# Weight operands of the second layer pair made once during the first, and Strassen's scheme for both products of all three pairs of blocks

## The chip, the cores and the metric

The kernel runs on one core of a Trainium2 chip. The metric is the device time of one execution in microseconds (us); lower is better. TensorE (PE) does the matrix products, VectorE (DVE), ScalarE (ACT) and GpSimd (POOL) the elementwise work, and SyncE (SP) issues the DMAs. Each engine works through its own list of instructions strictly in the order in which they were written into it; between engines, semaphores are waited on.

## The reference

```python
def reference(...):          # attention, then two feed-forward layers over 3072 tokens
    attn_out = _attn_ref(q, k, v, mem_k, mem_v)      # B=4, H=8, S=768, D=64; chunks of 32 with context and 8 memory keys
    x = attn_out.transpose(0, 2, 1, 3).reshape(B * S, H * D)          # 3072 x 512
    h = x @ moe_w_in                                                  # 512 -> 2048
    x = (h * clip(h + 3, 0, 6) / 6) @ moe_w_out                       # 2048 -> 512
    h = x @ moe2_w_in
    return maximum(0.01 * h, h) @ moe2_w_out
```

The weights come in as 64-bit floating point numbers, which the kernel decodes to 32-bit ones itself. Every 32-bit operand of a product is split into a high and a low part, and a product takes three matrix instructions: high by high, low weights by high, high by low.

## The kernel before

All work is in feature-major layout: a tile has 128 features on its partitions and 512 tokens in its row. The 3072 tokens are six blocks of 512. The first feed-forward layer goes block by block and, within a block, over 16 slices f of 128 hidden features. For each f, `hidden` issues 12 matmuls into a bank `h` (L647); then ACT writes the gate into `r` (L660), DVE multiplies (L663), ACT casts the high part of `g` (a call of `copy`, L291), and POOL or DVE subtracts to get the low part (`minus`, L294). `output` then issues 12 matmuls over the four banks `y` (L695) for the slice f - 1. So PE alternates: `h` of f + 1, `y` of f, `h` of f + 2, `y` of f + 1, each 12 matmuls of 512 columns. At a block's end `y_out` takes the four banks to SBUF tiles `ys` and writes them to the DRAM tensor `spill`. All 32 decoded and split weight tiles of the first layer stay in SBUF; the pool `w` has 33 places. While the first layer runs, the attention of later blocks is interleaved with it, and so is the decoding of the second layer's weights: `to_dram` decodes a slice (one ACT and four DVE instructions, L352 to L367) and writes it to DRAM.

The second layer takes the blocks in three pairs. Strassen's scheme (Winograd's form) computes a product of 2 x 2 blocks with seven block products instead of eight; its left operands are the three weight blocks a11, a12, a22 and four sums s1 to s4, its right operands three blocks of x and four sums t1 to t4 (`x_pair`, `x_quarter`). `seven` is the first product in this scheme for one pair p and one pair i of hidden slices, seven products of 6 matmuls (L977). `second` is the second product in the same scheme (L1114). Before the change `second` serves pairs 1 and 2 only: pair 0 uses `output` for both of its blocks, 12 matmuls for each block and each f. Pair 0 also makes the weight operands: `w_set` loads two decoded slices, forms the four sums and splits all seven operands, which pair 0 uses at once and which `keep` also writes to the DRAM tensor `kept` for the pairs 1 and 2; `w_more` does the same for the sums of the second product's weights during the first layer, and `w_static` writes their plain blocks during pair 0. Pairs 1 and 2 read each operand from `kept` through a ring of six `w` tiles (`left`).

The order on every engine is set before the launch by `schedule`: a list scheduler that plays the program through with assumed durations, lets each engine take the ready task with the lowest key, and gives out buffers as they come free in that play. Keys count matmuls in groups of four; a first-layer step f has 6 of them, and its `r` and `g` tasks have a key 12 below the step's own. A task whose key lies lower than that goes ahead of them.

```python
for f in range(KF):
    w32["2i", f] = to_dram("2i", w2i, f, B0 + 1.25 * BLK + 24 * f)
    w32["2o", f] = to_dram("2o", w2o, f, B0 + 1.25 * BLK + 24 * f + 12)
    if f % 2:
        w_more(f // 2, B0 + 1.25 * BLK + 24 * f + 32)
```

Of the kernel before, what the change touches and what calls it, by code (L numbers as in the profile page):

```python
# [35 lines left out]
N = 512  # L36
# [172 lines left out]
def tile_attn_moe_moe2(ctx: ExitStack, tc: tile.TileContext, raw, w1i, w1o, w2i, w2o, out):  # L209
# [41 lines left out]
    w2 = {n: dram.tile([KF, 128, 512], F32, name="w32" + n) for n in ("2i", "2o")}  # L251
    later = dram.tile([NT // (2 * N), KF, 128, N], F32, name="later")
# [59 lines left out]
    for p in range(PAIRED):  # L312
        if p:
            for i in range(KF // 2):
                seq2 += [("p", p, i, n) for n in FIRST]
                if i == 0 and p == 1:
                    seq2.append(("y", 1, KF - 1))
                seq2 += [("p", p, i, n) for n in THEN]
            seq2 += [("q", p, n, i) for n in FIRST + THEN for i in range(KF // 2)]
            continue  # L320
        for i in range(KF // 2):
            seq2 += [("p", p, i, n) for n in FIRST]
            if i == 0:
                seq2.append(("y", 2 * p - 1, KF - 1))
            else:
                seq2.append(("y", 2 * p, 2 * i - 2))
            seq2 += [("p", p, i, n) for n in THEN]
            if i:
                seq2.append(("y", 2 * p, 2 * i - 1))
        seq2 += [("y", 2 * p, KF - 2), ("y", 2 * p, KF - 1)]  # L330
        seq2 += [("y", 2 * p + 1, f) for f in range(KF - 1)]
    at = STEP * len(items)
    for kind, j, *of in seq2:
        if kind in "pq":
            (pos_p if kind == "p" else pos_q)[(j, *of)] = at
            at += 1.5
        else:
            if j >= 0:
                pos_y["2", j, of[0]] = at
            at += 3  # L340

    wbuf, wtask, w32 = {}, {}, {}

    def decode(src, f, key, early=None, after=(), place="wm"):
# [25 lines left out]
        k = add(absolute, {"ACT": act(512)}, key, after=[k], allocs=[m], uses=[t])  # L370
# [240 lines left out]
    wlast, ylast, ghi, rs = {}, {}, [], []  # L614
# [8 lines left out]
    def two_parts(lay, j, f, r, k, key, low, i=None):  # L623
        g = Buf("g")

        def of():
            return r.t if i is None else r.t[:, i]

        k = add(lambda e: copy(e, make(g)[:, 0, :], of()), {"ACT": act(N), "DVE": dve2(N)}, key, after=[k, *(ghi[-1:] if lay == "2" else [])], allocs=[g], uses=[r])
        ghi.append(k)  # L630
        k2 = add(lambda e: minus(e, g.t[:, 1, :], of(), g.t[:, 0, :].bitcast(F32)), low, key, after=[k], uses=[r, g])
        gbuf[lay, j, f, 0], gtask[lay, j, f, 0] = g, (k, k2)

    def hidden(lay, j, f, c0, n):
# [22 lines left out]
        wlast.setdefault((lay, "i", f), []).append(k)  # L657
# [17 lines left out]
    def output(lay, j, f, c0, n):  # L675
        t0 = blocks[j][0]

        halves = (KF // 2, KF) if lay == "1" and j < TWICE else (KF,)
        begin = c0 == 0 and f in (0, *halves)
        end = f + 1 in halves  # L680
        if begin:
            ybuf[lay, j] = banks_of(lay == "2" and (j // 2 + j) % 2 == 1)
# [26 lines left out]
        wlast.setdefault((lay, "o", f), []).append(ks[-1])  # L709
        ylast[lay, j, f] = ks[-1]  # L710
# [5 lines left out]
    def y_out(lay, j, f, t0, n, d, y, k, two):  # L716
        s = Buf("ys")
        key = pos_y[lay, j, f] - 12
        scale = 1.0 / 6.0 if lay == "1" else 1.0
        dst = (out if lay == "2" else spill)[d, :, t0:t0 + n]  # L720
# [15 lines left out]
        else:  # L736
            k = add(take, {"DVE": dve(n)} if d % 2 else {"ACT": act(n, 50.0)}, key, after=[k], allocs=[s], uses=[y])
# [77 lines left out]
    wop, wdone, chain, kdone = {}, {}, [], {}  # L815
# [7 lines left out]
    def sums_of(raws, sums, at, l, key):  # L823

        def part(name):
            if name in at:
                c, o = at[name]
                return raws[c].t[:, o:o + 256]
            c, o = {"s1": (0, 0), "s2": (0, 256), "s3": (1, 0), "s4": (1, 256)}[name]
            return sums[c].t[:, o:o + 256]  # L830

        def form(out, x, y, op, after, allocs=(), uses=()):
            def fn(e):
                for b in allocs:
                    make(b, ([128, 512], F32))
                engine(e).tensor_tensor(out=part(out), in0=part(x), in1=part(y), op=op)
            return add(fn, {"DVE": dve(256)}, key, after=after, allocs=allocs, uses=[*raws, *uses])

        s1 = form("s1", "a21", "a22", ALU.add, l, allocs=sums[:1])
        s2 = form("s2", "s1", "a11", ALU.subtract, [s1, l[0]], uses=sums[:1])  # L840
        s3 = form("s3", "a11", "a21", ALU.subtract, l, allocs=sums[1:])
        s4 = form("s4", "a12", "s2", ALU.subtract, [s2, s3], uses=sums)
        return s1, s2, s3, s4

    def load_raws(which, i, raws, key, after=()):
        out = []
        for c in range(2):
            def fn(e, c=c):
                nc.sync.dma_start(out=make(raws[c]), in_=w2[which][2 * i + c])
            out.append(add(fn, {"SP": dma(262144, 330.0)}, key, after=[w32[which, 2 * i], w32[which, 2 * i + 1], *after], allocs=[raws[c]]))  # L850
        return out

    def w_set(p, i, key):


        raws = [Buf("wm"), Buf("wm")]
        sums = [Buf("st"), Buf("st")]
        ts = [Buf("w") for _ in range(4)]
        gate = [pk[p, i - 1, 1]] if i else []
        l = load_raws("2i", i, raws, key - 16, chain)  # L860
        s1, s2, s3, s4 = sums_of(raws, sums, {"a11": (0, 0), "a12": (0, 256), "a21": (1, 0), "a22": (1, 256)}, l, key)

        def two(t, src, n, after):
            def fn_hi(e):
                make(ts[t], ([128, 2, 2, 256], F32R))
                copy(e, ts[t].t[:, 0].rearrange("p o c -> p (o c)")[:, :n], src.t[:, 512 - n:])

            def fn_lo(e):
                v = ts[t].t.rearrange("p h o c -> p h (o c)")
                minus(e, v[:, 1, :n], src.t[:, 512 - n:], v[:, 0, :n].bitcast(F32))  # L870

            hi = add(fn_hi, {"ACT": act(n)}, key + 0.5, after=after + gate, allocs=[ts[t]], uses=[src])
            lo = add(fn_lo, {"DVE": dve(n)}, key + 0.6, after=[hi], uses=[src, ts[t]])
            return hi, lo

        wop[p, i] = ts
        wdone[p, i] = d = [two(0, raws[0], 512, [l[0]]), two(1, sums[0], 512, [s1, s2]), two(2, sums[1], 512, [s3, s4]), two(3, raws[1], 256, [l[1]])]
        for q, n in enumerate(ORDER):
            c, o = IN_W[LEFT_OF[n]]
            keep("i", 7 * i + q, lambda c=c, o=o: ts[c].t[:, :, o], d[c], [ts[c]], key + 12)  # L880

    def w_more(i, key):


        raws = [Buf("wm"), Buf("wm")]
        sums = [Buf("ys"), Buf("ys")]
        l = load_raws("2o", i, raws, key - 8, chain)
        made_ = sums_of(raws, sums, {"a11": (0, 0), "a21": (0, 256), "a12": (1, 0), "a22": (1, 256)}, l, key)
        chain.clear()
        for q, n in enumerate(ORDER):  # L890
            name = LEFT_OF[n]
            if name[0] != "s":
                continue
            v = int(name[1]) - 1
            t, src, o = Buf("st"), sums[v // 2], 256 * (v % 2)

            def fn_hi(e, t=t, src=src, o=o):
                copy(e, make(t, ([128, 2, 256], F32R))[:, 0], src.t[:, o:o + 256])

            def fn_lo(e, t=t, src=src, o=o):  # L900
                minus(e, t.t[:, 1], src.t[:, o:o + 256], t.t[:, 0].bitcast(F32))

            hi = add(fn_hi, {"ACT": act(256)}, key + 0.5, after=[made_[v]], allocs=[t], uses=[src])
# [45 lines left out]
    def seven(p, i, n):  # L949


        if (p, i) not in held:
            held[p, i] = banks_of(p == 0 or i % 2), Buf("w"), {}
# [35 lines left out]
        if p:  # L989
            rlast[m] = [k]  # L990
# [305 lines left out]
```

## Time and profile before

| what | us |
|---|---|
| median of 3 runs (lowest, highest) | 1104.91 (1103.12, 1108.45) |
| time of the profiled execution | 1105.37 |
| its span, first to last instruction | 1103.6 |
| PE busy in the span | 1067.1 (97%) |
| DVE busy | 665.9 (60%) |
| ACT busy | 513.9 (47%) |
| POOL busy | 112.6 (10%) |
| DMA queue of the program, share of 16 engines | 59.7% |

The profile is of one execution. Its time is 1.8 us longer than its span and 0.5 us above the median. In rows of the timeline the first number is the start and the second the duration of an instruction, both in us; what is in square brackets is how long the engine stood idle before it and which instruction ended that. The duration of an instruction reaches until its results are written, and the next one on the same engine may start before that.

### The profile page before, as it was taken

How to read it: one execution, taken by the hardware profiler on the slowest of the kernel's cores; microseconds unless marked ns; L12 is line 12 of the kernel's file. 1: busy time of each engine (PE TensorE's matmuls, PEld its weight loads, DVE VectorE, ACT ScalarE, POOL GpSimd, SP SyncE). 2: the span in 40 equal slices, each digit the busy share in tenths (PEclk: the TensorE clock that was granted, in tenths of full speed). 3: DMA queues.
4: the chain of work that ended last, by engine and by line, in shares of the span. 5: the costliest groups of instructions: out<-in, count | busy, mean ns of one | idle time of the engine just before them, and what ended most of it. 6: DMA issues, size and time to landing. Idle time of an engine off the chain costs nothing.

```text
span 1103.6 us, 19815 instructions
## 1 busy us (share of the span) xinstructions
PE 1067.1 (97%) x7536; PEld 879.5 (80%) x7536; DVE 665.9 (60%) x1146; ACT 513.9 (47%) x1231; POOL 112.6 (10%) x112
## 2 busy tenths in 40 slices
PE   4599999999999999999999999999999999999998
PEld 3487888888888788888888888888888888888887
DVE  4698985635455444455676565657266696466573
ACT  4567554535555444354445344444234464233442
POOL 1030000002213212321222200000000000000000
PEclk8599999999999999999999999999999999999999
DMA  8886426625555644456455468897076787766763
GB/s 192 222 236 219 161 86 189 177 68 167 160 131 158 194 114 124 126 157 188 158 170 166 153 223 278 269 354 255 1 246 210 268 284 255 252 215 227 252 231 114
DMA packets 121055, 211.02 MB, mean 191 GB/s; under 512 B 11392, under 2 KB 64640, under 8 KB 120960
## 3 DMA queue, kind: packets, MB, share of 16 engines
q1 hardware_dynamic: 120960, 209.76, 59.7%
q8 instruction: 59, 0.97, 0.4%
q14 instruction: 36, 0.29, 0.1%
HBM read 148.90 MB, written 60.82 MB: 190 GB/s over the span
## 4 chain that ended last, share of the span: by engine, by line
PE 90%; DMA 5%; DVE 2%; SPq 1%; ACT 1%; issue 1%; DVEq 0%; ACTq 0%
PE y L695 26%; PE h L647 22%; PE hx L977 8%; PE y L977 7%; PE y L1114 6%; PE h L977 6%; PE hx L1114 4%; PE h L1114 4%; DMA w<-in_raw 2%; PE h L695 2%; PE hx L695 2%; PE at L523 1%; PE at L462 1%; DMA a<-in_raw 1%; SPq L427 1%; DMA w<-in_w1o 1%
## 5 line engine op out<-in xcount | busy, mean ns | idle before, releaser
L695 PE MATMUL y<-g,w 128*128 128x512 f32 x1344 | 327.7, 392 | 0.7 <-ACT ys L726 0.4
L695 PEld LDWEIGHTS y<-g,w 128*128 128x128 f32 x1344 | 251.2, 188 | 53.8 <-ACT ys L726 0.8
L647 PE MATMUL h<-xh,w 128*128 128x512 f32 x768 | 195.2, 395 | 1.6 <-ACT xh L291 1.6
L647 PEld LDWEIGHTS h<-xh,w 128*128 128x128 f32 x768 | 144.4, 190 | 32.2 <-ACT xh L291 2.0
L663 DVE SCALAR_TENSOR_TENSOR r<-r,h 128x512 f32<-128x512 f32 x96 | 65.9, 686 | 133.9 <-ACT r L660 133.7
L660 ACT ACTIVATE r<-h,three 128x512 f32<-128x512 f32 x96 | 66.5, 693 | 146.3 <-PE h L647 146.0
L294 POOL TENSOR_TENSOR g<-r,g 128x512 fp32r<-128x512 f32 x64 | 87.0, 1359 | 322.3 <-ACT g L291 309.0
L647 PE MATMUL h<-xl,w 128*128 128x512 f32 x384 | 104.5, 394 | 0.4 <-issue 0.4
L291 ACT CAST g<-r 128x512 fp32r<-128x512 f32 x111 | 69.3, 625 | 55.2 <-DVE r L663 48.9
L647 PEld LDWEIGHTS h<-xl,w 128*128 128x128 f32 x384 | 72.3, 190 | 15.9 <-issue 0.8
L294 DVE TENSOR_TENSOR w<-w 128x512 fp32r<-128x512 f32 (+1 forms) x108 | 70.2, 686 | 17.3 <-ACT w L291 16.4
L977 PE MATMUL hx<-w 128*128 128x512 f32 x288 | 69.3, 390 | 0.0
L291 ACT CAST g<-w 128x512 fp32r<-128x512 f32 x50 | 31.2, 623 | 78.8 <-PE hx L695 24.6
L977 PEld LDWEIGHTS hx<-w 128*128 128x128 f32 x288 | 54.0, 188 | 11.4 <-DVE ys L937 0.3
L944 ACT ACTIVATE w<-w 128x512 f32<-128x512 f32 x32 | 20.2, 632 | 88.0 <-DVE w L1028 66.5
L294 DVE TENSOR_TENSOR g<-w,g 128x512 fp32r<-128x512 f32 x50 | 34.4, 689 | 39.8 <-ACT g L291 39.8
L294 DVE TENSOR_TENSOR g<-r,g 128x512 fp32r<-128x512 f32 x48 | 34.6, 722 | 36.8 <-ACT g L291 33.2
L352 ACT ACTIVATE wm<-w 128x512 f32<-128x512 f32 x56 | 37.6, 673 | 25.7 <-DMA w<-in_w1i 11.1
L492 ACT ACTIVATE a<-at,mx 128x64 f32<-128x64 f32 x132 | 39.5, 335 | 18.9 <-DVE mx L480 18.9
L1114 PE MATMUL y<-w 128*128 128x512 f32 x204 | 47.9, 389 | 0.0
L363 DVE SCALAR_TENSOR_TENSOR wm<-w,wm 128x512 uint32<-128x512 uint32 x56 | 46.9, 837 | 1.1
L294 DVE TENSOR_TENSOR w<-wm,w 128x512 fp32r<-128x512 f32 (+1 forms) x58 | 40.7, 705 | 10.1 <-ACT w L291 8.9
(178 smaller groups left out, 1534.7 us busy)
## 6 DMA issues: line engine op xcount, KB each, us to landing
w<-kepti SPq DMA_DIRECT2D x56, 512.0 KB
w<-kepto SPq DMA_DIRECT2D x56, 512.0 KB
kepti<-w SPq DMA_DIRECT2D x56, 256.0 KB
a<-in_raw SPq DMA_DIRECT2D x44, 224.0 KB
w<-in_w1i SPq DMA_DIRECT2D x16, 512.0 KB
w<-in_w1o SPq DMA_DIRECT2D x16, 512.0 KB
w<-in_w2i SPq DMA_DIRECT2D x16, 512.0 KB
w<-in_w2o SPq DMA_DIRECT2D x16, 512.0 KB
```

The lines of the kernel that those rows point to most:

```text
L291: nc.scalar.copy(out, in_) if e == "ACT" else engine(e).tensor_copy(out=out, in_=in_)
L294: engine(e).tensor_tensor(out=out, in0=a, in1=b, op=ALU.subtract)
L352: nc.scalar.activation(out=make(m, ([128, 512], F32)), in_=t.t[:, :, 1].bitcast(F32), func=AF.Abs)
L363: nc.vector.scalar_tensor_tensor(out=mu, in0=t.t[:, :, 1], scalar=0xC0000000, in1=mu, op0=ALU.bitwise_and, op1=ALU.bitwise_or)
L492: nc.scalar.activation(out=e.t[:, i, r, :], in_=ps.t[:, r, i * W:(i + 1) * W], func=AF.Exp, bias=mx.t[:, r, i:i + 1], scale=1.0 / 8.0, acc ...
L647: nc.tensor.matmul(h.t[:, :n], w.t[:, 1 if p == 1 else 0, k * 128:(k + 1) * 128], x[:, k, c0:c0 + n], start=(p == 0 and k == 0), stop=(p = ...
L660: nc.scalar.activation(out=make(r)[:, :n], in_=h.t[:, :n], func=AF.Relu, bias=three[:, 0:1], scale=1.0)
L663: nc.vector.scalar_tensor_tensor(out=r.t[:, :n], in0=r.t[:, :n], scalar=6.0, in1=h.t[:, :n], op0=ALU.min, op1=ALU.mult)
L695: nc.tensor.matmul(bank(banks[d])[:, c0:c0 + n], w.t[:, 1 if p == 1 else 0, d * 128:(d + 1) * 128], g.t[:, 1 if p == 2 else 0, :n], start= ...
L944: return add(lambda e: nc.scalar.activation(out=at(), in_=at(), func=AF.Prelu, alpha=0.01), {"ACT": act(N)}, key, after=[after], uses=uses)
L977: nc.tensor.matmul(bank(to), w[:, kt * 128:(kt + 1) * 128], operand(p, name, 1 if q == 2 else 0, kt).bitcast(F32R), start=(fresh and q == ...
L1114: nc.tensor.matmul(bank(to[d]), w.t[:, o, 1 if q == 1 else 0, d * 128:(d + 1) * 128].bitcast(F32R), g.t[:, 1 if q == 2 else 0], start=(fre ...
```

## The change

Every left operand of the second layer pair, for both products, is now made in one place, `prepare`, while the first layer runs. There are 16 calls, alternately for the first and the second weights, each for one pair of slices: it loads and decodes two slices (64-bit numbers), splits the three plain blocks, forms the four sums in place in the two `wm` tiles, splits each, and writes all seven to `kept` through `ys` tiles (256 columns, high and low). Decoding of one call waits for the decoding of the one before. The calls have the keys 200 + 21k, where the decoding before had 120 + 24f for two slices. `to_dram`, `from_dram`, `w_set`, `w_more`, `w_static`, `again` and the tensors `w2` are gone. All three pairs now run `seven` and `second`, with weights from `kept` by the ring; `second` of pair 0 takes the place of the direct second product of blocks 0 and 1. For pair 0, the casts of the first six right operands of `second` wait until the fourth product of the last `seven` has been evacuated. The banks that `seven` and `second` start with are swapped, and at the end of the blocks 2 to 5 ACT alone takes the four `y` banks, where ACT and DVE took two each.

```diff
+PREPARE, EVERY = 200, 21
...
     for p in range(PAIRED):
-        if p:
-            for i in range(KF // 2):
...
-        seq2 += [("y", 2 * p, KF - 2), ("y", 2 * p, KF - 1)]
-        seq2 += [("y", 2 * p + 1, f) for f in range(KF - 1)]
+            if i == 0 and p == 0:
+                seq2.append(("y", -1, KF - 1))
             seq2 += [("p", p, i, n) for n in THEN]
+        seq2 += [("q", p, n, i) for n in FIRST + THEN for i in range(KF // 2)]
...
-        k = add(absolute, {"ACT": act(512)}, key, after=[k], allocs=[m], uses=[t])
+        k = add(absolute, {"ACT": act(512)}, key, after=[k, *gate], allocs=[m], uses=[t])
...
-            k = add(take, {"DVE": dve(n)} if d % 2 else {"ACT": act(n, 50.0)}, key, after=[k], allocs=[s], uses=[y])
+            k = add(take, {"DVE": dve(n)} if d % 2 and two else {"ACT": act(n, 50.0)}, key, after=[k], allocs=[s], uses=[y])
...
+    def prepare(which, src, i, key):
+        parts = [decode(src, 2 * i + c, key + 6 * c, after=splits[-2:], gate=chain) for c in range(2)]
+        raws, l = [m for m, _ in parts], [k for _, k in parts]
+        chain[:] = l
+        key += 12
...
+        def form(out, x, y, op, after):
+            return [add(lambda e: engine(e).tensor_tensor(out=part(out), in0=part(x), in1=part(y), op=op), {"DVE": dve(256)}, key, after=after, uses=raws)]
+
+        def parts_of(n, after):
+            t, b = Buf("ys"), raws[at[n][0]]
+            hi = add(lambda e: copy(e, make(t, ([128, 2, 256], F32R))[:, 0], part(n)), {"ACT": act(256)}, key, after=after, allocs=[t], uses=[b])
+            lo = add(lambda e: minus(e, t.t[:, 1], part(n), t.t[:, 0].bitcast(F32)), {"DVE": dve(256)}, key, after=[hi], uses=[b, t])
+            q = [LEFT_OF[m] for m in ORDER].index(n)
+            keep(which, 7 * i + q if which == "i" else KF // 2 * q + i, lambda: t.t, [hi, lo], [t], key + 2)
+            return [hi, lo]
+
+        d = {n: parts_of(n, l) for n in ("a22", "a11", "a12")}
+        s1 = form("s1", "a21", "a22", ALU.add, d["a22"])
+        s3 = form("s3", "a11", "a21", ALU.subtract, s1)
+        parts_of("s1", s1)
+        s2 = form("s2", "s1", "a11", ALU.subtract, s3 + d["a11"])
+        parts_of("s3", s3)
+        parts_of("s2", s2)
+        s4 = form("s4", "a12", "s2", ALU.subtract, s2 + d["a12"])
+        parts_of("s4", s4)
...
-            qbanks[p] = {m: [Buf(t), Buf(t)] for m, t in zip(FIRST, ("y", "y", "h", "hx"))} | {"ut": [Buf("w"), Buf("w")]}
+            qbanks[p] = {m: [Buf(t), Buf(t)] for m, t in zip(FIRST, ("h", "hx", "y", "y"))} | {"ut": [Buf("w"), Buf("w")]}
...
-        hi = add(lambda e: copy(e, make(g, ([128, 2, N], F32R))[:, 0], src()), {"ACT": act(N)}, key, after=ready + (quse[z - OPS:z - OPS + 1] if z >= OPS else []), allocs=[g], uses=[b])
+        hi = add(lambda e: copy(e, make(g, ([128, 2, N], F32R))[:, 0], src()), {"ACT": act(N)}, key, after=ready + (quse[z - OPS:z - OPS + 1] if z >= OPS else [c_of[p, KF // 2 - 1, "22"]]), allocs=[g], uses=[b])
...
-    for f in range(KF):
-        w32["2i", f] = to_dram("2i", w2i, f, B0 + 1.25 * BLK + 24 * f)
-        w32["2o", f] = to_dram("2o", w2o, f, B0 + 1.25 * BLK + 24 * f + 12)
-        if f % 2:
-            w_more(f // 2, B0 + 1.25 * BLK + 24 * f + 32)
+    for k in range(KF):
+        which, src = (("i", w2i), ("o", w2o))[k % 2]
+        prepare(which, src, k // 2, B0 + PREPARE + EVERY * k)
```

The first place is PE's list in pair 0, at the change from its first to its second product. Before, the direct product stands there: the last of block 0, then block 1 over the banks `h` and `hx`.

```order
407 L695 MATMUL y<-g,w 128x512 x12
408 L977 MATMUL h<-w 128x512 x6
409 L977 MATMUL hx<-w 128x512 x12
410 L695 MATMUL y<-g,w 128x512 x36
411 L695 MATMUL h<-g,w 128x512 x2
412 L695 MATMUL hx<-g,w 128x512 x2
413 L695 MATMUL h<-g,w 128x512 x2
414 L695 MATMUL hx<-g,w 128x512 x2
```

In the changed kernel the seven products of `second` follow there (L997), 48 matmuls each.

```order
385 L879 MATMUL h<-w 128x512 x6
386 L879 MATMUL hx<-w 128x512 x12
387 L879 MATMUL y<-xh,w 128x512 x6
388 L879 MATMUL y<-xl,w 128x512 x6
389 L879 MATMUL y<-w 128x512 x30
390 L997 MATMUL h<-g,w 128x512 x12
391 L997 MATMUL h<-w 128x512 x24
392 L997 MATMUL h<-g,w 128x512 x12
393 L997 MATMUL hx<-w 128x512 x24
394 L997 MATMUL hx<-g,w 128x512 x12
```

The 384 matmuls of `output` for blocks 0 and 1 have gone from the list, and 336 of `second` have come.

The second place is DVE's list in the last block of the first layer. Each row `r<-r,h` is the multiplication of one slice f; before, the rows 617, 623, 625 and 629 are those of f = 8 to 11, and little stands between them: sums and splits of `w_more`, and splits of weights read back.

```order
617 L663 SCALAR_TENSOR_TENSOR r<-r,h 128x512
618 L836 TENSOR_TENSOR ys<-wm 128x256 x2
619 L836 TENSOR_TENSOR ys<-ys,wm 128x256
620 L294 TENSOR_TENSOR st<-ys,st 128x256
621 L836 TENSOR_TENSOR ys<-wm,ys 128x256
622 L294 TENSOR_TENSOR st<-ys,st 128x256
623 L663 SCALAR_TENSOR_TENSOR r<-r,h 128x512
624 L294 TENSOR_TENSOR st<-ys,st 128x256
625 L663 SCALAR_TENSOR_TENSOR r<-r,h 128x512
626 L294 TENSOR_TENSOR w<-wm,w 128x512
627 L294 TENSOR_TENSOR st<-ys,st 128x256
628 L294 TENSOR_TENSOR w<-wm,w 128x512
```

In the changed kernel the rows between f = 9 (row 683) and f = 10 (row 701) are these; first ten of them, with the decoding of a slice (`wm<-wm` and `wm<-w,wm`, L338 to L350) and the sums and splits of pair 0's right operands (`x_quarter`, names with `a`):

```order
683 L630 SCALAR_TENSOR_TENSOR r<-r,h 128x512
684 L338 TENSOR_SCALAR wm<-wm 128x512
685 L292 TENSOR_TENSOR w<-a,w 128x512
686 L342 TENSOR_SCALAR wm<-wm 128x512
687 L292 TENSOR_TENSOR a<-a 128x512
688 L346 SCALAR_TENSOR_TENSOR wm<-w,wm 128x512
689 L292 TENSOR_TENSOR w<-w 128x512
690 L350 SCALAR_TENSOR_TENSOR wm<-w,wm 128x512
691 L292 TENSOR_TENSOR w<-a,w 128x512
692 L292 TENSOR_TENSOR a<-a,w 128x512
```

Then the last call of `prepare` (`ys<-wm,ys` are its splits, `wm<-wm` of 256 columns its sums), mixed with the rest of the right operands:

```order
693 L292 TENSOR_TENSOR ys<-wm,ys 128x256 x3
694 L805 TENSOR_TENSOR wm<-wm 128x256
695 L292 TENSOR_TENSOR xl<-w,xl 128x512
696 L805 TENSOR_TENSOR wm<-wm 128x256
697 L292 TENSOR_TENSOR ys<-wm,ys 128x256
698 L805 TENSOR_TENSOR wm<-wm 128x256
699 L292 TENSOR_TENSOR w<-a,w 128x512
700 L805 TENSOR_TENSOR wm<-wm 128x256
701 L630 SCALAR_TENSOR_TENSOR r<-r,h 128x512
```

Between the multiplications of f = 9 and f = 10 of the last block stand 19 instructions of DVE, where one stood before.

## Rows read from the trace of the kernel before

**Rows 1.** The page: busy time of PE; clock granted to PE in 40 slices.

```profile
PE 1067.1 (97%) x7536; PEld 879.5 (80%) x7536; DVE 665.9 (60%) x1146; ACT 513.9 (47%) x1231; POOL 112.6 (10%) x112
...
PEclk8599999999999999999999999999999999999999
```

**Rows 2.** Waits of PE from 109 us to the end: total, times, longest.

```profile
PE h L647 <- ACT xh L291: 1.6, 1, 1.6
PE y L695 <- ACT ys L726: 0.4, 1, 0.4
PE y L695 <- DVE ys L728: 0.2, 1, 0.2
```

**Rows 3.** The chain that ended last, merged pieces: start, duration, what.

```profile
109.83 3.96 PE h L647 x10
...
871.49 21.76 PE y L1114 x96
...
1100.01 0.69 DVE ys L937
```

**Rows 4.** PE's groups of the direct products, both layers: count, busy, mean ns.

```profile
L695 PE MATMUL y<-g,w 128*128 128x512 f32 x1344 | 327.7, 392 | 0.7 <-ACT ys L726 0.4 <-DVE ys L728 0.2
...
L695 PE MATMUL hx<-g,w 128*128 128x512 f32 x96 | 29.3, 390 | 0.0
L695 PE MATMUL h<-g,w 128*128 128x512 f32 x96 | 29.2, 389 | 0.0
```

**Rows 5.** Stretches: length, busy time of the engines, clock, DMA share, GB/s.

```profile
252.00:629.00 377.00, 376.33 (x3109) 309.77 (x3108) 205.05 (x347) 182.67 (x500) 93.00 (x70) 1.00 0.52 156
...
629.00:792.60 163.60, 163.60 (x723) 135.34 (x722) 93.70 (x160) 71.11 (x126) 1.08 (x1) 1.00 0.71 238
...
871.50:947.60 76.10, 76.10 (x337) 63.02 (x337) 58.28 (x94) 38.69 (x70) 0.00 (x0) 1.00 0.76 263
947.60:1023.80 76.20, 76.20 (x338) 63.11 (x337) 44.00 (x67) 27.54 (x45) 0.00 (x0) 1.00 0.64 224
```

**Rows 6.** Timeline of DVE, two instructions back to back, 512 columns.

```profile
879.31 0.69 DVE L294 TENSOR_TENSOR w<-a,w 128x512 fp32r<-128x512 f32 x1
879.91 0.69 DVE L294 TENSOR_TENSOR w<-w 128x512 fp32r<-128x512 f32 x1
```

**Rows 7.** Timeline of DVE, two instructions back to back, 256 columns.

```profile
594.51 0.42 DVE L836 TENSOR_TENSOR ys<-wm,ys 128x256 f32<-128x256 f32 x1
594.84 0.42 DVE L294 TENSOR_TENSOR st<-ys,st 128x256 fp32r<-128x256 f32 x1
```

**Rows 8.** DVE's groups of the decoding, by form: count, busy, mean ns.

```profile
L363 DVE SCALAR_TENSOR_TENSOR wm<-w,wm 128x512 uint32<-128x512 uint32 x56 | 46.9, 837 | 1.1
...
L367 DVE SCALAR_TENSOR_TENSOR wm<-w,wm 128x512 uint32<-128x512 uint32 x56 | 39.7, 708 | 1.0
...
L355 DVE TENSOR_SCALAR wm<-wm 128x512 f32<-128x512 f32 x56 | 26.2, 468 | 24.3 <-ACT wm L352 24.1
L359 DVE TENSOR_SCALAR wm<-wm 128x512 uint32<-128x512 uint32 x56 | 23.9, 426 | 1.4
```

**Rows 9.** Timeline of one first-layer step without delay: gate, cast, its y products.

```profile
450.44 0.69 ACT L660 ACTIVATE r<-h,three 128x512 f32<-128x512 f32 x1 [2.68 <-PE h L647]
...
451.88 0.62 ACT L291 CAST g<-r 128x512 fp32r<-128x512 f32 x1 [0.23 <-DVE r L663]
...
455.62 2.88 PE L695 MATMUL y<-g,w 128*128 128x512 f32 x12
```

**Rows 10.** Timeline of a step whose multiplication came late on DVE.

```profile
473.79 0.75 ACT L660 ACTIVATE r<-h,three 128x512 f32<-128x512 f32 x1
...
477.36 0.68 DVE L663 SCALAR_TENSOR_TENSOR r<-r,h 128x512 f32<-128x512 f32 x1
...
478.16 0.61 ACT L291 CAST g<-r 128x512 fp32r<-128x512 f32 x1
...
479.38 2.43 PE L695 MATMUL y<-g,w 128*128 128x512 f32 x10
```

More of the change, by code (lines that the diff above doesn't have):

```diff
@@ L621, in product, with two_parts @@
         return t
-    def two_parts(lay, j, f, r, k, key, low, i=None):
+    def two_parts(lay, j, f, r, k, key, low):
         g = Buf("g")
         def of():
-            return r.t if i is None else r.t[:, i]
-        k = add(lambda e: copy(e, make(g)[:, 0, :], of()), {"ACT": act(N), "DVE": dve2(N)}, key, after=[k, *(ghi[-1:] if lay == "2" else [])], allocs=[g], uses=[r])
-        ghi.append(k)
+            return r.t
+        k = add(lambda e: copy(e, make(g)[:, 0, :], of()), {"ACT": act(N), "DVE": dve2(N)}, key, after=[k], allocs=[g], uses=[r])
         k2 = add(lambda e: minus(e, g.t[:, 1, :], of(), g.t[:, 0, :].bitcast(F32)), low, key, after=[k], uses=[r, g])
@@ L676, in output @@
         t0 = blocks[j][0]
-        halves = (KF // 2, KF) if lay == "1" and j < TWICE else (KF,)
+        halves = (KF // 2, KF) if j < TWICE else (KF,)
         begin = c0 == 0 and f in (0, *halves)
@@ L718, in y_out @@
         key = pos_y[lay, j, f] - 12
[L719 to L720 removed]
+        scale = 1.0 / 6.0
+        dst = spill[d, :, t0:t0 + n]
         if two and f < KF - 1:
@@ L845, in load_raws @@
[L845 to L903, printed above, removed]
-            lo = add(fn_lo, {"DVE": dve(256)}, key + 0.6, after=[hi], uses=[src, t])
-            chain.append(lo)
-            keep("o", KF // 2 * q + i, lambda t=t: t.t, [hi, lo], [t], key + 2)
@@ L983, in seven @@
         us = [to, t, *xb]
-        product(part(0), N, [whi, *xhi, *need], allocs=alloc, uses=[u for u in us if u not in alloc], count=2)
-        product(part(1), N, [wlo], uses=us, count=2)
+        product(part(0), N, [wl, *xhi, *need], allocs=alloc, uses=[u for u in us if u not in alloc], count=2)
+        product(part(1), N, [], uses=us, count=2)
         k = product(part(2), N, xlo, uses=us, count=2)
@@ L1166, in second @@
                 ends(*{7: (1, 1), 3: (0, 1), 4: (1, 0)}[n], q, s)
-    def again(p, f, key):
-        if f % 2 == 0:
-            r = Buf("w")
-            before = pk[p, KF // 2 - 1, 4 if f else 7] if f < AGAIN else ylast["2", 2 * p + 1, f - AGAIN]
-            k = add(lambda e: nc.sync.dma_start(out=make(r, ([128, 2, N], F32)), in_=later[p, f:f + 2].rearrange("f p c -> p f c")), {"SP": dma(2 * N * 512, 330.0)}, key - 16, after=[held["b", p, f], held["b", p, f + 1], before], allocs=[r])
-            held["r", p, f] = r, k
-        r, k = held["r", p, f - f % 2]
-        two_parts("2", 2 * p + 1, f, r, k, key, {"DVE": dve(N)}, f % 2)
     B0 = pos_h["1", TWICE, 0] - TWICE * BLK
```

138 lines of the change are left out of this document (27 added, 111 removed).

## The prediction

> **What bounds the kernel now.** I read the page first. PE is busy for 97% of the span, and from the third slice of 40 on its clock row stands at 9, the full one [rows 1]. Nearly all of the other 3% lies in the first 110 us, which the change leaves as they are. Next the waits of PE behind 109 us: three, 2.2 us together in nearly 1000 us [rows 2]. So from 110 us on PE sets the end, and everything else is hidden behind it. The chain says the same: it is PE's matmuls up to 1099.98 us, then one DVE instruction of 0.69 us and the last write; and it gives the price of a matmul, 96 in 21.76 us, which is 226.7 ns [rows 3]. (The 390 ns of the groups overlap one another, so they are no price.) Two questions remain: how many matmuls go, and whether PE, which hardly waits now, begins to wait.
>
> **What goes.** `output` issues 1344 + 96 + 96 = 1536 matmuls [rows 4]. The first layer has six blocks of 16 slices of 12, which is 1152; the other 384 are the second product of pair 0. `second` needs seven products of eight pairs of slices of 6 matmuls, which is 336. The first product is in Strassen's form before and after. So 48 matmuls go: 48 x 226.7 ns = **10.9 us**. Pair 0, 163.6 us now (720 matmuls), becomes 672 matmuls, 152.3 us, like the two halves of 76.1 and 76.2 us that stand in the pairs 1 and 2 [rows 5].
>
> **What pair 0 gets.** Its weights come through the ring, as in the later pairs. There the DMA engines are 64 to 76% busy, and PE waits for no load [rows 2, 5]; pair 0 has 71% now and loses the reads and writes of `w_set`, `w_static` and `again`. I take 0; the cover is six operands loaded ahead. DVE has 58.3 us of work in a half of 76 us when it runs `second` [rows 5], so it keeps up there too. The first casts of `second` wait for the fourth product of the last `seven`. Behind it come three products, 18 matmuls or 4.1 us; an addition, a leak and a cast, each 0.6 to 0.7 us as the nearest rows show [rows 6, 9], take about 2 us. They are ready in time: 0, and about 1 us if each were twice as long. The four `y` banks at a block's end go through ACT alone: now PE waits 0.6 us in all for such evacuations [rows 2]; I take 0 of a possible further 0.6 us at each of three block ends, since the multiplication of the next slice need not wait for ACT's fourth copy. The exchange of banks costs nothing: both products alternate over the same eight.
>
> **What the first layer gets.** `prepare` splits three blocks and forms and splits four sums: 11 instructions of DVE with 256 columns in each of 16 calls, 176. Before, eight calls of `w_more` did four sums and four splits, 64. Back to back such an instruction takes 0.33 us [rows 7], so DVE gets 37 us more between 252 and 629 us, where it is busy 205 us of 377 [rows 5]: 54% becomes 64%. The decoding moves, but is the same in number. ACT gets 112 casts in place of 32; at no more than the 0.62 us of one with 512 columns [rows 9] that is at most 50 us, from 183 to 233 us of 377 [rows 5]. On average both are hidden. Whether they are hidden at each place is the question, because DVE's multiplication stands in the same list as the preparation and PE's `y` products need it.
>
> How late may it be? In an undelayed step the cast of `g` ends at 452.50 us and PE takes it at 455.62, 3.1 us later [rows 9]. In another the multiplication starts 2.8 us behind the end of its gate; the cast ends at 478.77 and PE goes on at 479.38 without a wait [rows 10]. So 3.1 to 3.4 us of delay cost nothing. A step of PE is 24 matmuls, 5.44 us.
>
> Now the order of the changed kernel, at the prices of before. One place stands out: from f = 9 to f = 10 of the last block, where the last call of `prepare` meets the right operands of pair 0. With the multiplication there are eight instructions of 512 columns at 0.60 us [rows 6], 4.8; eight of 256 at 0.33 [rows 7], 2.6; the decoding, 0.47 + 0.43 + 0.84 + 0.71 = 2.4 [rows 8]: 9.9 us for a step of 5.44. DVE is 4.4 us late, 1.3 more than there is room for. Nothing of this is urgent to PE, but DVE must pass it first. By the full durations of 0.69 and 0.42 us [rows 6, 7] it is 11.3 us and a stop of 2.8. The splits also wait for casts of ACT, which leans to the upper end; between 1.3 and 2.8 I take **2.0 us**, near the middle. The next heaviest steps, counted the same way, hold 7.1, 6.2 and 6.2 us: at most 1.7 us late, within the room. Where PE stops, the gates of the following `h` come later by the same time, so the lateness is paid once.
>
> [...]
>
> **The sum.** The profiled execution took 1105.4 us, 0.5 above the median of the runs, well inside their spread, so I correct nothing: 1105.4 - 10.9 + 2.0 = **1096.5 us**. The forecast's own range is 1095.5 to 1098.
>
> **Rivals.** *No stop at all*: 1105.4 - 10.9 = 1094.5 us. For it: DVE overlaps more than two rows show, and a delay of 2.8 us passed unseen [rows 10]. Against it: 9.9 us of work in 5.44 is far beyond.
>
> *The stop costs the clock too, or several stops come.* After the 1.6 us wait for a cast at the start of the dense stretch, ten matmuls took 3.96 us instead of 2.27 [rows 2, 3], 1.7 us more, about half the rate. With that behind a stop of 2 to 3 us the time is 1098 to 1099; with a longer spell at half rate, or a second stop at one of the steps of 6 to 7 us, up to 1102. Against it: PE had run in pieces before that wait [rows 1], and has 500 us of unbroken work before this one. [...]
>
> *Stops at four or more of the calls*, by waits between ACT and DVE that the prices don't hold: 1102 to 1110.
>
> *Slower: `prepare` runs in a lump each time.* A call's DVE work is 11 x 0.42 + 2 x 2.44 + the multiplication's 0.69 = 10.2 us [rows 6 to 8]. If all of it fell into one step, each call would be 4.8 us late, a stop of 1.7; sixteen make 27 us, and the time 1121. The gain is gone at 10.9 / 16 = 0.68 us a call. For it: the order is fixed beforehand, so no engine can step past a late instruction. Against it: the keys stand 21 apart, three and a half steps of 6, the order spreads most calls over such a stretch, and the bunch above is the only one of its size.
>
> **How the numbers follow.** Forecast (one stop, full clock) 0.42; no stop 0.20; clock or a second stop 0.20; several stops 0.10; the lump 0.05; 0.03 for below 1093.5. The range of 8 in 10 takes the first three: 1093.5 to 1102. A measurement of this kernel tells about 0.5% from no change, 5.5 us: 1099.4 and 1110.4. Faster: 0.42 + 0.20 + 0.03 and some 0.14 of the clock's 0.20, which is 0.79; the same: the other 0.06 and the several stops, 0.16; slower 0.05.
>
> **What the profile will show.** `second` with 1008 matmuls, 336 for each of three pairs, and `output` with 1152. Pair 0 in 152 us, with PE waiting for no ring load and not at the start of its `second`. One wait of PE for a cast `g`, 1.3 to 2.8 us, in the last third of the last first-layer block, about 600 us, behind a multiplication that starts more than 3 us after its gate; the granted clock behind it tells the second rival. DVE near 64% busy from 252 to 629 us. The prediction is wrong if PE waits for `g` at many calls of `prepare` (the lump), if a wait for a `w` of the ring appears in pair 0, or if PE has no wait at 600 us; and the gain is mis-sized if a matmul of `second` in pair 0 takes other than 226.7 ns.

## The result and the profile after

The changed kernel takes 1111.75 us (median of 20 runs, 1105.18 to 1114.36) against 1105.01 for the kernel before (20 runs): ratio 1.0054, interval 1.0040 to 1.0068. It is slower by half a per cent, where 1096.5 us and 0.8% faster had been forecast. The 20 times fall into two groups: four below 1107, and sixteen from 1109.97 on. The profile on hand is of the fastest, 1105.18 us; one of a common run comes with the first experiment.

The page: PE, and the clock granted to it in 40 slices.

```profile
PE 1061.6 (96%) x7488; PEld 872.8 (79%) x7488; DVE 707.5 (64%) x1230; ACT 532.0 (48%) x1297; POOL 114.2 (10%) x112
...
PEclk9999999999999999999999999999999999999999
```

There are 48 matmuls fewer, 7488 for 7536, as forecast. The windows of the two stretches in question, columns as in rows 5:

```profile
252.00:629.00 377.00, 367.70 (x2961) 299.94 (x2960) 247.69 (x445) 204.02 (x573) 90.80 (x67) 1.00 0.57 181
639.80:792.10 152.30, 152.30 (x674) 126.11 (x673) 99.74 (x158) 67.67 (x118) 0.86 (x1) 1.00 0.68 243
```

Pair 0 takes the forecast 152.3 us, with PE busy throughout. In the first layer PE now lacks 9.3 us of 377, where it lacked 0.7 [rows 5]. The waits of PE from 109 us on:

```profile
PE y L662 <- ACT g L289: 5.3, 2, 4.6
PE y L662 <- ACT ys L691: 2.8, 2, 2.3
PE at L482 <- POOL a L478: 0.7, 1, 0.7
PE at L482 <- DVE a L478: 0.5, 1, 0.5
```

Against rows 2 there are two new stops of more than 1 us. The larger is where the order let expect one, at the `y` products of f = 10 of the last block. The timeline there, first DVE from the multiplication of f = 9 to that of f = 10 (in part), then ACT, PE and POOL:

```profile
601.71 0.68 DVE L630 SCALAR_TENSOR_TENSOR r<-r,h 128x512 f32<-128x512 f32 x1
...
603.25 1.52 DVE L342 TENSOR_SCALAR wm<-wm 128x512 uint32<-128x512 uint32 x1
...
612.19 0.68 DVE L630 SCALAR_TENSOR_TENSOR r<-r,h 128x512 f32<-128x512 f32 x1
...
599.17 0.41 ACT L289 CAST ys<-wm 128x256 fp32r<-128x256 f32 x1 [0.56 <-DMA kepti<-ys]
599.48 0.69 ACT L627 ACTIVATE r<-h,three 128x512 f32<-128x512 f32 x1
...
602.49 0.62 ACT L289 CAST g<-r 128x512 fp32r<-128x512 f32 x1
...
605.93 0.68 ACT L627 ACTIVATE r<-h,three 128x512 f32<-128x512 f32 x1
...
612.90 0.62 ACT L289 CAST g<-r 128x512 fp32r<-128x512 f32 x1 [2.15 <-DVE r L630]
...
596.61 1.07 PE L615 MATMUL h<-xl,w 128*128 128x512 f32 x4
...
603.16 3.04 PE L662 MATMUL y<-g,w 128*128 128x512 f32 x12
...
613.57 4.50 PE L662 MATMUL y<-g,w 128*128 128x512 f32 x12 [4.65 <-ACT g L289]
...
603.19 1.30 POOL L292 TENSOR_TENSOR g<-r,g 128x512 fp32r<-128x512 f32 x1 [5.56 <-PE h L615]
```

The two multiplications are 10.48 us apart, near the 9.9 of the prediction: DVE loses 5.0 us on a step of PE. But the stop is 4.65 us, not 1.3 to 2.8, because the 3.1 us of room were gone before the bunch began. For f = 9 the cast of `g` ended at 603.11 and PE took it at 603.16. Two delays had used the room up. The gate of f = 9 began at 599.48, 1.8 us after the last matmul of its `h` ended (597.68), behind a cast of `prepare` that waited for a `ys` tile; and the multiplication began at 601.71, 1.5 us after the gate's end. (The gate of f = 10 came late too, at 605.93, but it ended 5.6 us ahead of the multiplication, which DVE's list held up.) The L342 in the middle took 1.52 us; its like take 0.43; it lies beside POOL's subtraction of 603.19. Behind the stop, twelve matmuls took 4.50 us instead of the usual 2.88: the granted clock from 613.5 to 616.8 us was 0.51, where it was 1.00 from 603.0 to 606.5 us and again from 616.8 to 629.0 us.

The smaller stop is at the end of block 3, which had been priced at 0 of a possible 0.6 us. ACT, then PE:

```profile
455.11 0.69 ACT L627 ACTIVATE r<-h,three 128x512 f32<-128x512 f32 x1 [2.60 <-PE h L615]
...
456.55 0.62 ACT L289 CAST g<-r 128x512 fp32r<-128x512 f32 x1 [0.75 <-DVE r L630]
457.07 1.08 ACT L691 ACTIVATE ys<-y 128x512 f32<-128x512 f32 x2
...
457.71 2.59 PE L662 MATMUL y<-g,w 128*128 128x512 f32 x9 [2.25 <-ACT ys L691]
```

ACT's third and fourth bank stand in its list behind the next slice's gate, which waits 2.60 us for `h`, and that slice's cast, which waits 0.75 us for DVE. So PE, which needs the third bank, waits 2.25 us.

### The profile page after: what moved, and what is told of

The parts are those of the page before. It is cut to its first block, busy times and chain, and to the rows that moved or that the text cites. A ratio compares the mean times of both kernels' runs of the same rounds, so it can differ in the third digit from the quotient of the medians.

```text
span 1103.4 us, 19981 instructions
## 1 busy us (share of the span) xinstructions
PE 1061.6 (96%) x7488; PEld 872.8 (79%) x7488; DVE 707.5 (64%) x1230; ACT 532.0 (48%) x1297; POOL 114.2 (10%) x112
## 4 chain that ended last, share of the span: by engine, by line
PE 77%; DVE 7%; DMA 7%; ACT 3%; SPq 2%; issue 2%; POOL 0%; ACTq 0%; DVEq 0%
PE y L662 17%; PE h L615 17%; PE y L997 12%; PE y L879 10%; PE h L997 6%; PE hx L879 6%; PE h L879 4%; PE hx L997 3%; DMA w<-in_raw 2%; DMA a<-in_raw 2%; DMA w<-in_w1o 2%; DVE ys L292 1%; PE at L493 1%; SPq L397 1%; DVE wm L346 1%
## 5 line engine op out<-in xcount | busy, mean ns | idle before, releaser
L662 PE MATMUL y<-g,w 128*128 128x512 f32 x1152 | 283.8, 393 | 8.1 <-ACT g L289 5.3
L662 PEld LDWEIGHTS y<-g,w 128*128 128x128 f32 x1152 | 216.2, 189 | 56.5 <-ACT g L289 6.6
L292 DVE TENSOR_TENSOR w<-w 128x512 fp32r<-128x512 f32 (+1 forms) x162 | 105.5, 687 | 17.4 <-ACT w L289 16.5
L854 ACT ACTIVATE w<-w 128x512 f32<-128x512 f32 x48 | 30.3, 632 | 132.1 <-DVE w L911 100.2
L997 PE MATMUL y<-w 128*128 128x512 f32 x384 | 90.0, 389 | 0.0
L289 ACT CAST g<-r 128x512 fp32r<-128x512 f32 x97 | 60.5, 624 | 58.2 <-DVE r L630 53.3
L997 PEld LDWEIGHTS y<-w 128*128 128x128 f32 x384 | 72.1, 188 | 15.0
L292 DVE TENSOR_TENSOR ys<-wm,ys 128x256 fp32r<-128x256 f32 x112 | 61.2, 568 | 20.4 <-ACT ys L289 20.2
L879 PE MATMUL y<-w 128*128 128x512 f32 x264 | 61.8, 389 | 0.0
L289 ACT CAST w<-w 128x512 fp32r<-128x512 f32 x102 | 58.3, 618 | 6.2 <-DVE w L292 4.5
L879 PEld LDWEIGHTS y<-w 128*128 128x128 f32 x264 | 49.6, 188 | 10.3
L289 ACT CAST ys<-wm 128x256 fp32r<-128x256 f32 x112 | 41.8, 410 | 23.5 <-DVE wm L350 14.6
```

The source lines that it names most:

```text
L289: nc.scalar.copy(out, in_) if e == "ACT" else engine(e).tensor_copy(out=out, in_=in_)
L292: engine(e).tensor_tensor(out=out, in0=a, in1=b, op=ALU.subtract)
L662: nc.tensor.matmul(bank(banks[d])[:, c0:c0 + n], w.t[:, 1 if p == 1 else 0, d * 128:(d + 1) * 128], g.t[:, 1 if p == 2 else 0, :n], start= ...
L854: return add(lambda e: nc.scalar.activation(out=at(), in_=at(), func=AF.Prelu, alpha=0.01), {"ACT": act(N)}, key, after=[after], uses=uses)
L879: nc.tensor.matmul(bank(to), t.t[:, o, l, kt * 128:(kt + 1) * 128].bitcast(F32R), operand(p, name, 1 if q == 2 else 0, kt).bitcast(F32R), ...
L997: nc.tensor.matmul(bank(to[d]), w.t[:, o, 1 if q == 1 else 0, d * 128:(d + 1) * 128].bitcast(F32R), g.t[:, 1 if q == 2 else 0], start=(fre ...
```

## The experiments

Each time is compared with runs of the kernel before on the same chip. "First layer" is the stretch of the profiled execution from PE's first matmul of the 17th slice to that of the last slice of block 5, the same 79 slices in every kernel, read from the timeline. (The blocks 0 and 1 go in halves, so the 17th slice is f = 8 of block 0.) From there to PE's last matmul it is 475.9 us before the change and 464.9 in every kernel after it: 11.0 us less, in each of them.

| kernel | median us | ratio (interval) | profiled execution | its first layer, us |
|---|---|---|---|---|
| before | 1104.7 to 1105.5 | 1 | 1105.37 | 469.0 |
| the change | 1111.75 | 1.0054 (1.0040 to 1.0068) | 1105.18 | 482.2 |
| 1: the same again | 1112.05 | 1.0059 (1.0038 to 1.0080) | 1111.77 | 486.6 |
| 2: y by ACT and DVE | 1108.88 | 1.0029 (1.0014 to 1.0044) | 1101.72 | 477.5 |
| 3: key 180 | 1102.20 | 0.9969 (0.9956 to 0.9983) | 1098.42 | 474.7 |
| 4: 2 and 3 | 1101.94 | 0.9972 (0.9956 to 0.9988) | 1103.66 | 478.2 |
| 5: one subtraction to DVE | 1107.00 | 1.0017 (1.0004 to 1.0030) | 1108.06 | 483.7 |
| 6: key 54 | 1105.99 | 1.0005 (0.9993 to 1.0017) | 1108.55 | 482.7 |
| 7: 2, 6, nine subtractions | 1097.52 | 0.9927 (0.9904 to 0.9950) | 1100.40 | 472.0 |
| 8: 3, 6, all subtractions | 1097.25 | 0.9926 (0.9903 to 0.9948) | 1095.44 | 472.5 |
| 9: before, all subtractions | 1105.42 | 1.0010 (1.0002 to 1.0019) | 1107.47 | 471.6 |
| 10: all subtractions alone | 1092.76 | 0.9888 (0.9874 to 0.9901) | 1091.76 | 467.9 |
| 11: 8 and 2 | 1098.07 | 0.9930 (0.9918 to 0.9942) | 1098.07 | 472.1 |
| 12: 11 with key 190 | 1092.50 | 0.9886 (0.9871 to 0.9901) | 1092.65 | 468.0 |

The profiled executions also begin differently (PE reaches the 17th slice between 152.0 and 157.1 us), so the last column is what compares two of them.

**1. The change once more.** No edit.

> The changed kernel once more, with a profile. Theory A (the gain of 48 matmuls is there in full, and stops of PE in the first layer give it back): PE without a stop from 640 us on, pair 0 in 152.3 us; between 250 and 630 us stops of 9 to 17 us in all, the longest near 600 us behind DVE's list, and one near 455 us behind ACT's evacuations of y; in a run of 1111 us the 6 us more than in the profile of 1105 lie there too, as longer stops or as half clock behind them. Theory B (the loss is outside the first layer: loads of the ring, the start): the stops between 250 and 630 us are the same 9 us, and the 6 us lie before 110 or after 630 us.

This execution took 1111.77 us and belongs to the common group (the six times run from 1108.50 to 1116.13, so the gap between the groups is not a clean one). Its first layer is 17.6 us longer than before; with 11.0 us gained behind it and a start 0.4 us earlier that makes 6.1 us more, which is the difference in PE's last matmul (1105.73 for 1099.58). Theory A holds in the main: against the first profile, 4.4 of the 6.6 us lie in the first layer. The other 2.1 lie ahead of the 17th slice (154.25 for 152.11 us), in the start, which B had named. What is new in the first layer is one row of POOL. POOL, then DVE from the multiplication of f = 9 on (in part), the cast of f = 9 on ACT, then PE:

```profile
598.25 1.28 POOL L292 TENSOR_TENSOR g<-r,g 128x512 fp32r<-128x512 f32 x1 [3.35 <-ACT g L289]
605.12 9.08 POOL L292 TENSOR_TENSOR g<-r,g 128x512 fp32r<-128x512 f32 x1 [5.59 <-PE h L615]
...
603.62 0.68 DVE L630 SCALAR_TENSOR_TENSOR r<-r,h 128x512 f32<-128x512 f32 x1
...
605.15 0.42 DVE L342 TENSOR_SCALAR wm<-wm 128x512 uint32<-128x512 uint32 x1
...
612.99 0.68 DVE L630 SCALAR_TENSOR_TENSOR r<-r,h 128x512 f32<-128x512 f32 x1
613.59 1.16 DVE L292 TENSOR_TENSOR w<-a,w 128x512 fp32r<-128x512 f32 x1
...
604.41 0.64 ACT L289 CAST g<-r 128x512 fp32r<-128x512 f32 x1
...
605.10 2.12 PE L662 MATMUL y<-g,w 128*128 128x512 f32 x8
614.26 2.08 PE L662 MATMUL y<-g,w 128*128 128x512 f32 x4 [7.04 <-POOL g L292]
```

POOL's subtraction, the low part of `g` for f = 9, takes 9.08 us instead of 1.28, and PE stops for 7.04 us. Through these 9 us DVE has no pause and takes its operands from SBUF alone. POOL is done 1.21 us after DVE's next instruction with an operand in PSUM (`r<-r,h` at 612.99) begins, which is about what the subtraction before it took (1.28 us). But a list of DVE without a pause does not always go with a long row of POOL. In the first profile the same subtraction began in the same place of the same unbroken list, 0.06 us ahead of DVE's L342 (603.19, 603.25); there L342 took 1.52 us and POOL 1.30. Here it began 0.03 us ahead (605.12, 605.15), and L342 took 0.42 us and POOL 9.08. The windows show the granted clock, 1.00 during the row and 0.51 from 612 us on:

```profile
606.00:612.00 6.00, 1.22 (x6) 0.66 (x4) 6.00 (x14) 3.25 (x7) 6.00 (x1) 1.00 0.27 101
612.00:619.00 7.00, 4.74 (x11) 3.74 (x12) 2.75 (x5) 0.00 (x0) 2.20 (x1) 0.51 0.17 66
```

**2. y's banks by ACT and DVE**, as before the change.

```diff
-            k = add(take, {"DVE": dve(n)} if d % 2 and two else {"ACT": act(n, 50.0)}, ...
+            k = add(take, {"DVE": dve(n)} if d % 2 else {"ACT": act(n, 50.0)}, ...
```

> Only the evacuation of y is undone: ACT and DVE take two banks each at the ends of the blocks 2 to 5. Theory A: the 2.8 us of waits of y for ys (2.3 of them near 455 us) shrink to below 0.7, the stop near 600 us stays at 4 to 6 us; 2 to 4 us below the unchanged one, about 1107 to 1109. Theory B: no difference beyond 1 us.

The waits for `ys` fall from 2.8 to 0.7 us, the 4.6 us for `g` stay, and the median is 3.2 us below that of experiment 1: theory A's figure. The profile is of this kernel's fastest run.

**3. The first call of `prepare` 20 keys earlier.**

```diff
-PREPARE, EVERY = 200, 21
+PREPARE, EVERY = 180, 21
```

> Only the key of the first prepare goes from 200 to 180: the last call no longer meets the right operands of pair 0; by the order no step of DVE holds more than 7.1 us at the prices of before. Theory A: the stop near 600 us and its half clock are gone, 6 us or more below the unchanged one: 1099 to 1105. A rival within A (DVE is short of time in the whole stretch, not at one place): the stop comes at another step, and the time stays within 2 us of the unchanged one. Theory B: no difference.

9.9 us below experiment 1, as A forecast. The last call still meets pair 0's right operands, but spread over more steps: the longest way there from one multiplication to the next is 6.8 us (592.02 to 598.82). What is left near 600 us is again a row of POOL, of 4.42 us, and PE's 2.4 us behind it:

```profile
600.22 4.42 POOL L292 TENSOR_TENSOR g<-r,g 128x512 fp32r<-128x512 f32 x1 [5.36 <-ACT g L289]
...
604.70 1.20 PE L662 MATMUL y<-g,w 128*128 128x512 f32 x4 [2.36 <-POOL g L292]
```

**4. Both.** The edits of 2 and 3.

> Both: key 180, and y by ACT and DVE. Theory A: the gain of 10.9 us nearly whole, stops below 3 us in all: 1094.5 to 1098. The rival within A: 1103 to 1109. Theory B: as the unchanged one.

Not 1095 to 1098: no better than 3. POOL's 2.4 us stay, and at the end of block 2 PE waits 3.5 us for a bank that DVE takes late, with a granted clock of 0.56 from 367.2 to 370.6 us behind it (nine matmuls in 3.69 us). The edits do not add up; each makes the planner write another order.

**5. One subtraction to DVE.** Theory P is now: POOL's row of 9.08 us came from DVE's list without a pause beside it.

```diff
-... {"DVE": 600.0} if j < TWICE else {"POOL": pool(n), "DVE": dve(n)})
+... {"DVE": 600.0} if j < TWICE or (j, f) == (5, 9) else {"POOL": pool(n), "DVE": dve(n)})
```

> The changed kernel; one instruction alone changes its engine: the low part of g of f = 9 in the last block goes from POOL to DVE. Theory P (POOL's subtraction is kept from its operands as long as DVE runs without a pause, so it lasted 9.08 us in a run of 1111.8 and 1.30 in one of 1105.2): no subtraction of POOL over 3 us near 605 us, PE's stop there falls from 7 to about 4.6 us, one spell of half clock in place of two, and the time to 1105 to 1108, with hardly a run over 1110. Theory Q (DVE's lateness alone; POOL's long row stands beside it): DVE gets 0.6 us more in the bunch, the stop is the same or 0.6 us longer, 1111 to 1113.

PE's list is the same as in the change, and DVE's differs in 13 rows. The median falls by 5 us, to 1107.0; one of 12 runs is above 1109, where 21 of the 26 runs of the change are. PE's waits:

```profile
PE y L662 <- ACT g L289: 4.8, 2, 4.1
PE y L662 <- ACT ys L691: 2.8, 2, 2.3
```

There is no wait for POOL, and the lateness of DVE stays with 4.1 us. The fastest run of the change looked like this too, so it is the 12 times, more than the one profile, that speak for P and against Q. The bunch and POOL's row are two causes, one on top of the other.

**6. Pair 0's right operands 12 keys later**, `prepare` as in the change.

```diff
-                x_pair(p, pos_p[p, 0, 1] - 66, 18)
+                x_pair(p, pos_p[p, 0, 1] - 54, 18)
```

> The changed kernel; only the key of pair 0's right operands is 54 instead of 66 ahead of its first product, so that they follow the last call of prepare instead of mixing with it; prepare stays where it is. By the order no step of the last block then holds more than 5.5 us of DVE. If the meeting of the two is the cause (P and Q): the stop near 600 us below 1.5 us, no half clock there, 1100 to 1104 (the stops at 360 and 455 us stay). If DVE is short of time in the whole stretch, or the calls of prepare as such cost: a stop elsewhere and 1109 to 1112. If pair 0 then waits for its right operands: a wait of PE behind 640 us.

1105.99, above what was expected. No step of the last block is as heavy, the wait for `g` is 0.9 us at most; but a subtraction of POOL is long again, 5.08 us, one slice later. POOL, DVE and PE:

```profile
613.51 5.08 POOL L292 TENSOR_TENSOR g<-r,g 128x512 fp32r<-128x512 f32 x1 [2.96 <-ACT g L289]
...
617.39 0.67 DVE L630 SCALAR_TENSOR_TENSOR r<-r,h 128x512 f32<-128x512 f32 x1
...
618.65 2.08 PE L662 MATMUL y<-g,w 128*128 128x512 f32 x4 [2.29 <-POOL g L292]
```

It ends 1.20 us after the multiplication at 617.39 begins, as in experiment 1 (and in 3: 1.21 us after the one at 603.43; and in 4, where 4.41 us end 1.20 us after the one at 608.67). A lighter list of DVE doesn't keep POOL's rows short.

**7. The three causes together.** Edits of 2 and 6, and the subtractions of f = 7 to 15 of the last block on DVE.

> Key 54, the low parts of g of f = 7 to 15 of the last block on DVE, and y's banks by ACT and DVE: the three causes found so far mended together. Theory P: stops between 250 and 640 us below 3 us in all, 1095 to 1100. If a cause is missing: 1101 or more, and its stop stands in the trace.

1097.52, within P's range; PE's waits past 112 us are 1.6 us together.

**8. No subtraction on POOL.** Edits of 3 and 6, and:

```diff
-... {"DVE": 600.0} if j < TWICE else {"POOL": pool(n), "DVE": dve(n)})
+... {"DVE": 600.0})
```

> Keys 54 and 180, and every low part of g on DVE, none on POOL; y by ACT alone. Theory P: the 44 instructions of DVE that lasted over 0.2 us longer than their like (39.8 us together, each beside one of POOL) are like the others, so DVE's busy time in the first layer is about the same although 64 subtractions come on top; 1096 to 1101. Rival: they are long for another reason and stay, DVE is overloaded at several steps (up to 7.4 us by the order): 1103 to 1110.

1097.25, as P expected. The window of 252 to 629 us:

```profile
252.00:629.00 377.00, 375.07 (x3003) 308.08 (x3003) 245.81 (x500) 204.72 (x573) 10.85 (x8) 1.00 0.56 178
```

DVE has 55 rows more than in the change (500 for 445) and is busy 1.9 us less. In the change, 44 of its instructions there lasted over 0.2 us longer than the median of their like, 39.8 us together, and each of the 44 overlapped one of POOL; here 4 do, with 3.4 us. So here the subtractions that POOL took over cost DVE about as much as doing them. (Key 180 moves other rows in and out of the window; with the change's own keys, in experiment 10, DVE has 65 rows more and is busy 3.6 us more.) One stop stays, 1.9 us for banks near 358 us.

**9. The kernel before, without subtractions on POOL.** The edit of 8.

> The kernel before the change, with every low part of g of the first layer on DVE and none on POOL. Theory P: the 32 instructions of DVE that last over 0.2 us longer than their like between 252 and 629 us (27.5 us together) nearly vanish, DVE's busy time there stays within 12 us of 205, and the time does not move (within 2 us of 1105), because PE had no stop to lose there. If POOL's subtractions as such cost time in any kernel: 1 us or more faster.

The instructions of DVE that last over 0.2 us longer than their like go from 32 (27.5 us) to 2 (0.8 us), DVE's busy time from 205 to 213.7 us, and the time does not get better: 1.0010. Before the change PE hardly waited for DVE, 0.2 us behind 109 us [rows 2], so these 27.5 us cost it next to nothing. A stop that was not there before comes with it, 1.4 us for a bank that DVE takes late near 362 us.

**10. The change with the edit of 8 alone.**

> The changed kernel with its own keys and ACT alone for y, but every low part of g on DVE. By the order the heaviest step of the last block then holds 8.4 us of DVE instead of 10.1 (the calls of prepare fall otherwise). Theory P: no wait of PE for a low part, the stop near 600 us below 1.5 us, the waits for y's banks stay at 2 to 3 us; 1098 to 1102. Theory Q (the meeting of prepare and the right operands alone counts): still 4 us or more of stop near 600 us, 1105 or more.

1092.76 us, 1.1% below the kernel before and 19 us below the change; 5 us below P's range. PE has no wait past the start of the dense stretch:

```profile
PE h L615 <- ACT xh L289: 1.6, 1, 1.6
```

And in the window it is busy throughout:

```profile
252.00:629.00 377.00, 377.00 (x3079) 311.00 (x3062) 251.29 (x510) 208.93 (x580) 8.44 (x7) 1.00 0.55 177
```

The waits for y's banks are gone too, with ACT alone taking them: with other assumed engines the planner writes another order, and near 449 us ACT now takes the three last banks in one go, ahead of the next gate. So this run shows that the change is worth its forecast when PE is fed, not how much of the 19 us belongs to which cause. Experiments 2, 3 and 5 give 3.2, 9.9 and 5 us, each alone, and these do not add up (experiment 4).

**11. Experiment 8 with y by ACT and DVE.**

> Keys 54 and 180, every low part of g on DVE, y's banks by ACT and DVE. Against the same with ACT alone (1097.3 us, whose profile has 1.9 us of waits for y's banks near 360 us and a spell of half clock behind them): if these waits cost it 2 to 3.5 us, 1094 to 1096; if DVE, now with two banks more, brings its own wait there (3.5 us in the run with key 180 alone), 1097 or more.

1098.07, the second case: PE waits 1.0 and 0.3 us for banks near 361 us, with a granted clock of 0.50 from 363.0 to 366.4 us behind.

**12. The same with key 190.**

> The same with key 190 for the first prepare. The stops near 360 us depend on which instruction of a call stands ahead of the evacuation; the other places are as before. 1094 to 1098; a difference of more than 2 us to the one with 180 would lie near 360 or 455 us.

1092.50, a little below the range: no wait at all behind the start, as in 10. The 5.6 us to experiment 11 lie near 361 us (4.0 us of first layer) and in the start. Both kernels have every subtraction on DVE, so in the first layer it is the order alone that makes the difference.

## Why the prediction was wrong

**The gain was right.** 48 matmuls, 10.9 us forecast; 11.0 us less behind the first layer in every kernel, and a median 12.0 us lower in experiment 10 (which also loses 1.2 us of gaps of before). Pair 0's ring, the gate on its casts and the swap of banks cost nothing, as said.

**The stop was at the right place and too small.** The step that failed is the room: "DVE is 4.4 us late, 1.3 more than there is room for", and with it "between 1.3 and 2.8 I take 2.0". DVE's lateness itself was priced about rightly, 5.0 us in the first profile (10.48 - 5.44) and 3.9 in the common run (9.37 - 5.44). But the 3.1 us of room had been read from a step without delay, and here they were spent when the bunch began: at f = 9 PE took the cast 0.05 us after its end, in both profiles. So the lateness became a stop nearly whole, 4.65 us. The low part of `g` on POOL, for which the sum has no term, was taken for finished in time; in the common run it is what ends the stop, 7.0 us. And the clock added its share, as the second rival said, 1.6 us in the first profile and 2.3 in the common one (the granted clock was 0.51 there in both; the rows behind the stops against 2.88, 1.07 and 1.98 us at 1.00). Together the steps there cost 6.8 us in the first profile and 11.4 in the common run (8.5 and 2.9 us over the same steps of the kernel before), where 2.0 had been taken. DVE's instructions were priced from undisturbed rows too: in the first profile 44 of them, each beside an instruction of POOL, took about 0.9 us more than their like (39.8 us together), though in the bunch this is one row, the L342 (1.52 us for 0.43).

**"I take 0" for y's banks on ACT alone** was wrong by 3.2 us (experiment 2): the argument looked at the next slice's multiplication, and not at where the third copy stands in ACT's list.

**The sum, mended:** 11.0 gained; 17.6 us lost in the first layer of the common run, of which 11.4 near 600 us, 2.8 near 455, 1.3 near 358, 1.0 near 580 (each over the same steps of the kernel before), and some 1.1 in small gaps. That leaves 6.6 us more, and 1111.75 was measured against 1105.01.

**The rivals.** The nearest in kind is the second: a second stop came, though at a block's end, and half clock behind the first; but together they cost more than its 1102. "Stops at four or more of the calls" comes nearest in time (1102 to 1110) by the wrong cause: one place and one block's end made most of it. The lump did not come: experiments 10 and 12 run all 16 calls without a stop. The three signs that were to tell the prediction wrong did not appear either; none of them was a stop at the forecast place that is too long. No rival had DVE and POOL lengthen each other's instructions, and with that goes the common run's longest wait, the 7.04 us for POOL's row of 9.08 (about 5 us of the median by experiment 5; without it the change is still not faster). In the change's profile 87 instructions of DVE between 252 and 629 us overlap one of POOL; the 44 slow ones are all among them. The other way round, four rows of POOL took 9.08, 5.08, 4.42 and 4.41 us, each beside a whole row of DVE's instructions and not beside one alone, where the median of POOL's subtractions in the change's profile is 1.29 us. What the two engines get in each other's way over is not shown.

## What to carry to other kernels

Before work is added to DVE's list in a stretch where GpSimd feeds TensorE, price both against each other: look for instructions of either that take longer beside one of the other (here 44 of DVE's by about 0.9 us, and one of POOL's with 9.08 us for 1.28), and for places where DVE would run without a pause. Here the subtractions moved to GpSimd saved DVE next to nothing (experiment 8: 55 rows more on DVE, busy 1.9 us less). With none moved, experiments 10 and 12 ran without a stop, while 8 and 11 kept one near 360 us, so the order counts as well. In a kernel with fixed orders, read the room for lateness across the whole chain (gate, multiplication, cast, low part), on each engine's list, and at the step that gets the work: room seen in an undelayed step may have been spent by the steps ahead.

## What was not expected of the hardware

The same program ran with POOL's subtraction at 1.30 us in one execution and at 9.08 in another; their first layers differ by 4.4 us. It began 0.06 us ahead of DVE's L342 in the one and 0.03 us ahead in the other; what decides between the two is not shown. That this also makes the two groups of times is not shown, as one execution of each has a profile; experiment 5 speaks for it. The four long rows of POOL ended 1.21, 1.20, 1.21 and 1.20 us after DVE began an instruction that reads PSUM (`r<-r,h`). And the clock after a stop was not the same each time: behind the 2.25 us at a block's end it stayed at 1.00 in the change's profile and was 0.51 a little later in experiment 5; behind 1.37 us in experiment 9 it was 0.50.
